# A fused attention and gated-MLP kernel on one core: low parts shared with Pool, turned h from the accumulator, last group on DVE, new tables

## The chip, the cores and the metric

The kernel runs on one core of a Trainium2 chip. The time is that of the device, in microseconds (us), median of several executions. Names of engines: PE is TensorE, ACT ScalarE, DVE VectorE, Pool GpSimd. The mean clock of TensorE, as a share of full speed, is listed for each execution.

## The reference, cut to what matters

```python
def mab(q, kv):                                  # attention of 32 rows over all, or of all over 32
    s = scale * (q @ kv.transpose(0, 2, 1))
    a = np.exp(s - s.max(-1, keepdims=True)); a /= a.sum(-1, keepdims=True) + 1e-09
    return a @ kv
h = mab(I, x)                                    # x: 4 batches of 12416 x 128, I: 32 x 128
x = mab(x, h)
g = x @ w_gate                                   # 128 x 1536
out = x + sigmoid(x @ w_res) * (gelu(g) * (x @ w_val) @ w_out)
```

The kernel never forms the second attention's result ahead of the MLP: with `h` only 32 rows, `h @ w_gate` and `h @ w_val` are made once a batch (`hgv`), and each block of tokens multiplies its 32 weights (`rt`) into them. Batch 0 has nothing to hide behind, so its `h` is made in a prologue, during which no gelu runs.

## The kernel before: the parts that matter here

Each tile of x (1024 tokens) is split into a float16 high part and a float16 low part, is turned on PE, gets its exponentials on ACT, and is accumulated on PE. In the prologue the high parts are cast on DVE or ACT, and all low parts are subtracted on DVE:

```python
def convert_hi(b, k, eng):                       # act: a Copy; else tensor_copy, float32 -> float16
    ...
def convert_lo(b, k, eng):
    po.memset(lo[:, :w, P:P + 1], 1.0)
    eng.tensor_tensor(lo[:, :w, :P], xf, hi, AL.subtract)     # two SBUF inputs
...
for n in range(ntile + 2):
    hi_next(n + 1)                               # ACT for odd tiles below 10, else DVE
    if n < ntile:
        convert_lo(0, tiles[n], ve)
        turn_pe(0, tiles[n])                     # 8 transpositions on PE, copied out by ACT
    if 1 <= n <= ntile: exps("a", 0, ...)        # tile n - 1
    if n >= 2:
        if n == ntile + 1: weight_cast(0, ve); weight_cast(1, ve)
        accumulate(0, ...)                       # tile n - 2; DVE copies the end result to nacc
finish_h(0)      # PE folds nacc; DVE reciprocal and scaling; Pool makes hra of it
turn_h(0)        # PE transposes, DVE copies: ht
for i in range(2, 5): weight_cast(i, po)
exps("b", 0, 0, half, bank_v())
first_layer(0, 0, act)
...
act.activation(gel, parts, AC.Gelu, ...)         # brings the gelu table in (1.28 us on ACT at 35.34)
warm = bank_f()
for i in range(10):
    pe.matmul(warm, wG[:, :P], wG[:, :TOK], start=True, stop=True)
```

The main part is a list of words that say in what order PE, ACT and DVE get their work ("the tables"). A group of 512 tokens ends with `th * ffn + at`, partly on DVE, partly by way of ACT and Pool:

```python
if on_act:
    act.activation(fe, f, AC.Copy, ...)
    po.tensor_tensor(th, th, fe, AL.mult); po.tensor_tensor(at, at, fe, AL.add)
else:
    ve.scalar_tensor_tensor(th, th, 1.0, f, AL.add, AL.mult)
po.tensor_tensor(at, at, th, AL.add)
sy.dma_start(out[...], at)
```

The softmax here doesn't subtract the row's maximum and nothing guards it: scores larger than these inputs give would overflow.

## Time and profile before

| | before |
|---|---|
| median time, range of the first three executions | 776.06 us (775.07 to 777.73) |
| accumulator read by DVE (nacc) | 27.54 us |
| ht begins | 29.40 us |
| first gelu | 37.22 us |
| last product on PE ends | 768.40 us |
| span of the profile | 773.1 us |

The table is read as five points of one road. The stretch to nacc is the first stage, from nacc to the first gelu the second, then come 731.2 us of main part, which is 1164 gelus at 0.63 us each, and a tail of 4.7 us. As a first reading, what delays the first gelu delays everything, because in the main part ACT and DVE are both full (from 200 to 300 us ACT is busy 99.94 of the 100 us, DVE 97.73). The lines for this are in the prediction below.

### The profile page before, as it was taken

To read this page: it belongs to the slowest core of one execution; us is meant where nothing else is said; L and a number is where in the kernel's file an instruction comes from. 1 tells how busy PE (TensorE), PEld (TensorE's weight loads), DVE (VectorE), ACT (ScalarE), POOL (GpSimd) and SP (SyncE) were. 2 spreads that over 40 slices of the span, in tenths; PEclk is the share of its full clock that TensorE was granted. 3 is DMA by queue.
4 is the path that set the end of the run, shared out by engine and by line. 5 is a ranking of instruction groups with operands and counts; after the bars stand their busy time and mean duration, and the time that the engine had idled before them with its cause. 6 is when DMAs were issued, how large, how long until landed. Compare 5 with 4: busy or idle time off the path is not lost.

```text
span 773.1 us, 23909 instructions
## 1 busy us (share of the span) xinstructions
PE 736.8 (95%) x9590; PEld 431.0 (56%) x9590; DVE 742.4 (96%) x737; ACT 754.2 (98%) x1505; POOL 462.5 (60%) x466
## 2 busy tenths in 40 slices
PE   5799999999999999999999999999999999999997
PEld 4555555555655555565655555556565554655554
DVE  7799999989999999999999999998999999999997
ACT  6799999999999999999999999999999999999997
POOL 0238989713598886833377896872267871434155
PEclk9999999999999999999999999999999999999999
DMA  8325596510245675620124485560106341110101
GB/s 339 120 49 122 145 217 162 142 59 29 50 79 117 146 187 149 175 66 30 43 64 99 107 217 144 152 156 29 38 21 129 87 86 43 42 43 29 43 31 58
DMA packets 118449, 78.16 MB, mean 101 GB/s; under 512 B 96672, under 2 KB 99392, under 8 KB 118336
## 3 DMA queue, kind: packets, MB, share of 16 engines
q1 hardware_dynamic: 118336, 76.62, 38.7%
q8 instruction: 75, 1.23, 0.6%
q14 instruction: 38, 0.31, 0.1%
HBM read 27.87 MB, written 25.43 MB: 69 GB/s over the span
## 4 chain that ended last, share of the span: by engine, by line
ACT 43%; PE 39%; issue 11%; DVE 5%; DMA 1%; POOL 1%; SPq 0%; ACTq 0%; POOLq 0%; DVEq 0%
ACT ge L368 29%; PE f L391 18%; PE g L357 10%; PE v L357 6%; ACT th L405 3%; ACT at L410 3%; DVE u L362 3%; PE g L399 3%; ACT e L166 2%; ACT xt L141 1%; ACT fe L419 1%; ACT L166 1%; ACT hi L116 1%; ACT L368 1%; DMA ge<-in_x_dram 1%
## 5 line engine op out<-in xcount | busy, mean ns | idle before, releaser
L362 DVE TENSOR_TENSOR u<-ge,v 128x1024 bf16<-128x1024 f32 x584 | 670.6, 1212 | 10.3 <-PE v L357 2.7
L368 ACT ACTIVATE ge<-g 128x512 f32<-128x512 f32 x1164 | 609.1, 657 | 2.7 <-PE g L357 1.2
L391 PEld LDWEIGHTS <-u 128*128 128x128 bf16 x4656 | 270.1, 98 | 207.8 <-issue 203.4
L391 PE MATMUL f<-wO,u 128*128 128x128 bf16 x4656 | 370.4, 220 | 4.3 <-ACT fe L419 1.1
L357 PE MATMUL g<-rt,hgv 32*128 32x512 f16 x1152 | 335.9, 379 | 9.3 <-ACT ge L368 0.6
L357 PE MATMUL v<-rt,hgv 32*128 32x512 f16 x1152 | 222.9, 385 | 2.5 <-DVE u L362 1.6
L424 POOL TENSOR_TENSOR at<-at,th 128x512 f32<-128x512 f32 (+1 forms) x100 | 124.0, 1240 | 148.2 <-DVE th L423 52.0
L357 PEld LDWEIGHTS <-hgv 32*128 32x128 bf16 x2400 | 73.7, 91 | 87.8 <-issue 24.2
L420 POOL TENSOR_TENSOR th<-th,fe 128x512 f32<-128x512 f32 (+1 forms) x35 | 41.3, 1180 | 94.4 <-ACT fe L419 94.4
L294 POOL TENSOR_TENSOR a<-e,z 128x1024 f16<-128x1024 f32 (+1 forms) x48 | 89.7, 1880 | 12.3 <-DVE z L280 7.8
L124 POOL TENSOR_TENSOR lo<-xf,hi 128x1024 f16<-128x1024 f32 x36 | 76.9, 2136 | 0.2
L399 PE MATMUL g<-hra,rt 128*128 128x128 f16 x768 | 71.3, 219 | 2.5
L405 ACT ACTIVATE th<-g 128x512 f32<-128x512 f32 (+1 forms) x100 | 64.1, 649 | 0.3 <-PE g L399 0.2
L410 ACT ACTIVATE at<-g 128x512 f32<-128x512 f32 (+1 forms) x100 | 64.3, 651 | 0.0
L399 PEld LDWEIGHTS <-rt 128*128 128x128 f16 x768 | 50.7, 97 | 16.1 <-issue 13.1
L118 POOL CAST hi<-xf 128x1024 f16<-128x1024 f32 x36 | 37.3, 1037 | 16.9 <-DMA xf<-in_x_dram 12.5
L423 DVE SCALAR_TENSOR_TENSOR th<-th,f 128x512 f32<-128x512 f32 x65 | 44.4, 683 | 2.5 <-PE g L162 1.8
L421 POOL TENSOR_TENSOR at<-at,fe 128x512 f32<-128x512 f32 (+1 forms) x35 | 41.3, 1179 | 0.0
L162 PEld LDWEIGHTS <-xt 128*128 128x128 f16 x768 | 23.0, 97 | 7.3 <-issue 3.4
L419 ACT ACTIVATE fe<-f 128x512 f32<-128x512 f32 (+1 forms) x35 | 22.1, 631 | 0.9 <-PE f L391 0.9
L273 POOL TENSOR_TENSOR a<-a 128x256 f32<-128x256 f32 (+5 forms) x45 | 18.6, 413 | 3.5
L207 POOL CAST hra<-nacc 64x128 f16<-64x128 f32 x4 | 1.1, 288 | 29.3 <-DVE nacc L200 29.3
(114 smaller groups left out, 280.0 us busy)
## 6 DMA issues: line engine op xcount, KB each, us to landing
out_dram<-at SPq DMA_DIRECT2D x96, 256.0 KB, 2.2
xf<-in_x_dram SPq DMA_DIRECT2D x38, 512.0 KB, 4.5
ge<-in_x_dram SPq DMA_DIRECT2D x10, 512.0 KB, 8.3
rt<-a SPq DMA_TRANSPOSE x48, 3.2
xt<-hi SPq DMA_TRANSPOSE x36, 3.4
ge<-in_moe_w_gate_dram SPq DMA_DIRECT2D x1, 512.0 KB, 8.4
ge<-in_moe_w_val_dram SPq DMA_DIRECT2D x1, 512.0 KB, 8.5
ge<-in_moe_w_out_dram SPq DMA_DIRECT2D x1, 512.0 KB, 4.2
```

The source lines that it names most:

```text
L124: eng.tensor_tensor(lo[:, :w, :P], xf_t.pop((b, k))[:, :w, :], hi_t[b, k][:, :w, :], AL.subtract)
L294: eng.tensor_tensor(a2[:, :n], ev[:, o:o + n, :].unsqueeze(2).to_broadcast([P, n, Q, M]), z[:, o:o + n].unsqueeze(2).unsqueeze(3).to_broad ...
L357: pe.matmul(*t[n], start=True, stop=True)
L362: ve.tensor_tensor(u[:, :n], ge_t.pop(value)[:, :n], v_t.pop(value)[:, :n], AL.mult)
L368: act.activation(ge_t[i][:, h * TOK:h * TOK + n], gb[:, :n], AC.Gelu, bias=0.0, scale=1.0)
L391: pe.matmul(self.ffn[:, k, :], u_t[self.gi, si][:, o:o + P], wO[:, fc, :], start=first, stop=not self.todo, skip_group_check=True)
L399: pe.matmul(bank[:, k * P:(k + 1) * P], rt_t[self.b, self.k][:, self.j0 + k, :], hra_t[self.b][:, s, :], start=True, stop=True)
L405: act.activation(self.th[:, :self.tw], self.mix(0), AC.Tanh, bias=0.0, scale=0.5)
L410: act.activation(self.at[:, :self.tw], self.mix(1), AC.Copy, bias=0.0, scale=1.0)
L420: po.tensor_tensor(th, th, fe, AL.mult)
L423: ve.scalar_tensor_tensor(th, th, 1.0, f, AL.add, AL.mult)
L424: po.tensor_tensor(at, at, th, AL.add)
```

## The change

Its intent was to shorten the prologue by balancing three engines, to shorten the tail, and to anneal the tables once more. The diff, cut (the copy helper of `turn_pe`, the other engine arguments and the 75 rows of tables are left out):

```diff
+    def turned_h(b):
+        hs = bank_g(); na = nacc_t[b]
+        pe.matmul(hs[:, :M], na[:, P:P + 1].to_broadcast([P, P]), strips[:, 0, :], ...)
+        pe.matmul(hs[:, P:2 * P], na[:, :P], strips.rearrange("p q m -> p (q m)"), ...)
+        ve.reciprocal(rz, hs[:, :M])
+        ve.tensor_tensor(ht, hs[:, P:2 * P], rz (broadcast), AL.mult)
...
-            po.tensor_tensor(at, at, th, AL.add)
+            (ve if self.gi == ngrp - 1 else po).tensor_tensor(at, at, th, AL.add)
...
-            convert_hi(0, tiles[n], act if n % 2 and n < 10 else ve)
+            convert_hi(0, tiles[n + 1], ve)
-            convert_lo(0, tiles[n], ve)
+            convert_lo(0, tiles[n], po if w == PRE and n % 2 and n < ntile - 1 else ve)
...
-    finish_h(0)
-    turn_h(0)
+    weight_cast(0, act)
+    weight_cast(1, act)
+    turned_h(0)
     for i in range(2, 5):
         weight_cast(i, po)
-    exps("b", 0, 0, half, bank_v())
-    first_layer(0, 0, act)
+    exps("b", 0, 0, half, bank_g())
+    finish_h(0)
+    first_layer(0, 0)                  # its copy now on DVE
...
-    for i in range(10):
+    for i in range(6):
         pe.matmul(warm, ...)
...
-                lasts.pop(0).end(on_act[lg.gi])
+                lasts.pop(0).end(on_act[lg.gi] and lg.gi < ngrp - 1)
```

Accumulation also runs three tiles behind instead of two.

More of the change, by code (lines that the diff above doesn't have):

```diff
@@ L132, in turn, with turn_pe @@
                                hi_t[b, k][:, :w, :].rearrange("p k c -> p (k c)"))
-    def turn_pe(b, k):
+    def turn_pe(b, k, both=False):
         _, w = blocks_of(k)
@@ L137, in turn_pe @@
         xt_t[b, k] = xt
+        if both:
+            for j0, eng in ((0, act), (w // 2, ve)):
+                tps = bank_g().bitcast(FP16).rearrange("p (k c) -> p k c", c=P)
+                for j in range(j0, j0 + w // 2):
+                    pe.transpose(tps[:, j - j0, :], hi_t[b, k][:, j, :], identF)
+                if eng is act:
+                    act.activation(xt[:, j0:j0 + w // 2, :], tps[:, :w // 2, :], AC.Copy,
+                                   bias=0.0, scale=1.0)
+                else:
+                    eng.tensor_copy(xt[:, j0:j0 + w // 2, :], tps[:, :w // 2, :])
+            return
         tps = bank_g().bitcast(FP16).rearrange("p (k c) -> p k c", c=P)
@@ L210, in finish_h @@
         hgv_t[b] = p_h.tile([P, F], BF16, name="hgv", tag="hgv")
+    def turned_h(b):
+        hs = bank_g()
+        na = nacc_t[b]
+        pe.matmul(hs[:, :M], na[:, P:P + 1].to_broadcast([P, P]), strips[:, 0, :],
+                  start=True, stop=True)
+        pe.matmul(hs[:, P:2 * P], na[:, :P], strips.rearrange("p q m -> p (q m)"),
+                  start=True, stop=True)
+        rz = p_h.tile([P, M], FP32, name="rzt", tag="rzt", bufs=1)
+        ve.reciprocal(rz, hs[:, :M])
+        ht = p_h.tile([P, P], FP16, name="ht", tag="ht")
+        ve.tensor_tensor(ht.rearrange("p (q m) -> p q m", m=M),
+                         hs[:, P:2 * P].rearrange("p (q m) -> p q m", m=M),
+                         rz.unsqueeze(1).to_broadcast([P, Q, M]), AL.mult)
+        ht_t[b] = ht
     def turn_h(b):
@@ L217, in turn_h, with first_layer @@
         ht_t[b] = ht
-    def first_layer(b, c, eng):
+    def first_layer(b, c):
         bank = bank_g()
@@ L222, in first_layer @@
             pe.matmul(bank[r, :], ht_t[b][:, r], w[:, c:c + TOK], start=True, stop=True)
-        if eng is act:
-            act.activation(hgv_t[b][:, c:c + TOK], bank, AC.Copy, bias=0.0, scale=parts)
-        else:
-            ve.tensor_scalar(hgv_t[b][:, c:c + TOK], bank, parts, None, op0=AL.mult)
+        ve.tensor_scalar(hgv_t[b][:, c:c + TOK], bank, parts, None, op0=AL.mult)
     def first_layer_t(b, s):
@@ L248, in spread, with res_layer @@
                                a2[:, :n].rearrange("p c q m -> p (c q m)"))
-    def res_layer(b):
+    def res_layer(b, eng=act):
         bank = bank_g()
@@ L253, in res_layer @@
         hra = hra_t[b]
-        act.activation(hra[:64, 0, :], bank[:64, :P], AC.Copy, bias=0.0, scale=1.0)
+        if eng is act:
+            act.activation(hra[:64, 0, :], bank[:64, :P], AC.Copy, bias=0.0, scale=1.0)
+        else:
+            eng.tensor_copy(hra[:64, 0, :], bank[:64, :P])
         ve.tensor_tensor(hra[M:2 * M, 0, :], bank[M:2 * M, :P], hra[M:2 * M, 0, :], AL.subtract)
@@ L484, in weight_cast @@
         dst, src, w = pieces[i]
-        eng.tensor_copy(dst, staged.pop(i)[:, :w])
+        if eng is act:
+            act.activation(dst, staged.pop(i)[:, :w], AC.Copy, bias=0.0, scale=1.0)
+        else:
+            eng.tensor_copy(dst, staged.pop(i)[:, :w])
     for i in range(len(pieces)):
         weight_in(i)
-    def hi_next(n):
+    convert_hi(0, tiles[0], ve)
+    for n in range(ntile + 3):
+        if n + 1 < ntile:
+            convert_hi(0, tiles[n + 1], ve)
         if n < ntile:
-            convert_hi(0, tiles[n], act if n % 2 and n < 10 else ve)
-    hi_next(0)
-    for n in range(ntile + 2):
-        hi_next(n + 1)
-        if n < ntile:
-            convert_lo(0, tiles[n], ve)
-            turn_pe(0, tiles[n])
+            w = blocks_of(tiles[n])[1]
+            convert_lo(0, tiles[n], po if w == PRE and n % 2 and n < ntile - 1 else ve)
+            turn_pe(0, tiles[n], n == ntile - 1 and w == PRE)
         if 1 <= n <= ntile:
@@ L503 @@
             exps("a", 0, n0, n0 + w, bank_v())
-        if n >= 2:
-            if n == ntile + 1:
-                weight_cast(0, ve)
-                weight_cast(1, ve)
-            n0, w = blocks_of(tiles[n - 2])
-            accumulate(0, n0, n0 + w, n == 2, n == ntile + 1)
-    finish_h(0)
-    turn_h(0)
+        if n >= 3:
+            n0, w = blocks_of(tiles[n - 3])
+            accumulate(0, n0, n0 + w, n == 3, n == ntile + 2)
+    weight_cast(0, act)
+    weight_cast(1, act)
+    turned_h(0)
     for i in range(2, 5):
@@ L514 @@
     half = PRE // 2
-    exps("b", 0, 0, half, bank_v())
-    first_layer(0, 0, act)
+    exps("b", 0, 0, half, bank_g())
+    finish_h(0)
+    hf_t.pop(0)
+    first_layer(0, 0)
     exps("b", 0, half, WIDE, bank_v())
-    later = [(t0, min(t0 + WIDE, nblk)) for t0 in range(WIDE, nblk, WIDE)]
-    exps("b", 0, *later[0], bank_v())
+    exps("b", 0, WIDE, 2 * WIDE, bank_v())
     sums_b(0, 0, half, ve)
@@ L522 @@
     weights_b(0, 0, 0, half, ve, True)
-    for j0, j1 in later[1:]:
-        exps("b", 0, j0, j1, bank_v())
-    first_layer(0, TOK, ve)
-    first_layer(0, 2 * TOK, ve)
-    res_layer(0)
+    first_layer(0, TOK)
+    for j0 in range(2 * WIDE, nblk, WIDE // 2):
+        exps("b", 0, j0, min(j0 + WIDE // 2, nblk), bank_g())
+    first_layer(0, 2 * TOK)
+    res_layer(0, ve)
     sums_b(0, half, WIDE, ve)
@@ L532 @@
         weight_cast(i, po)
+    later = [(t0, min(t0 + WIDE, nblk)) for t0 in range(WIDE, nblk, WIDE)]
     gel = konst.tile([P, 1], FP32, name="gel")
@@ L536 @@
     warm = bank_f()
-    for i in range(10):
+    for i in range(6):
         pe.matmul(warm, wG[:, :P], wG[:, :TOK], start=True, stop=True)
     plan_first = [
-        "GGQGG GVG4 P6 P4 GV R8VG",
-        "G5GQG 7AQ6 RP8A GP6 GQ2 4GQ *",
-        "7P8G Q8 GQ13R P8 4P 5Q",
-        "R7P 8P10 AA6GP 4GQ7 P8 P10",
-        "GGGV 9GQ2G 8RP 1P7 P A8P7G",
-        "Q 13GP 12P Q8GG 7P3 1Q",
-        "R5PA P11 P4 A9V GP5GG 6P",
-        "8P 5A4P QR 10PR 10GP QA14",
-        "P11 QG8 GGV6 GG9RQG 5GQ9 GQ9",
-        "GVG 7GVGR9 GQA9GG Q 5P5G VR10",
-        "P10 P 18EV VEE2Ac cQ5 P *",
-        "10GQ7GG Q7G GV6G Q11AG Q12 P7G",
-        "V G6P4R 7P 6P G6GP Q4R7 *",
-        "P7G Q4A4 V GA9GGV 13PG 7Q",
-        "6GP6 P7 P7G Q8 RR7P A8P",
-        "8GQ 8GQ9A 3P8 R4GQG1 5P6 QG7",
-        "GVG7G Q7A 4P5 R6GP2 GQ7 GQ7GG",
-        "V17EE E15EcP 6cP Q9AR4 P5 GVA7G",
-        "Q6 GGV11 GGcP Q8R P7G P7 *",
-        "QG7 GQ6R 5QG 8hP 4P6A 5GtQ",
-        "QG9l G1QG 6Q G4A7P 6P lGV5RR",
-        "8P 7P7rG V 21EEAV EEEEVE6 9PG17",
-        "GoQ6 QG8 R2GQoG 5VGG 6P5A 6P *",
-        "R8VG G6GVG 12oPG11 oGQ7 GQ5 2P7",
-        "GVG 7A4P5G *",
+        "GGPG P5 P3 GQ8 GGV7GG Q6",
+        "VGR3 2P 7P A7QGG Q8RA 8P",
+        "7P 7P9A P9R GP5 P6 P5G *",
+        "V8 RP11 QG11 2PG 10P7 P10",
+        "R1P8 P8A 4PA5G Q7 Q GQG6GG",
+        "V G5VGG 8P 8GV GR9GGVG QR13A",
+        "GQ5 VGG 8P 9P7G G6Q QA6",
+        "A7GQ 10GQG 9QG7 GG9RVG G5QG9 QG9",
+        "P8 P8 AR9P Q9 GG5Q G7GGV",
+        "6VGG8 GVG3A 10QG GQ3 R10P7 GQ2R",
+        "10P 16EV V E6EcP 6cQ P5G *",
+        "4P 6GVG 6P3A10 2P Q11 R5P",
+        "6P7 P8 AP3 R8PG5G Q7 GQ7G",
+        "VGA9 GQ8 GQ4R 8P PA8 P5",
+        "GGV 8R3P3 Q G7GGV6GG8AG Q6 P3",
+        "6P10 VGG10G Q3A 10GP3G VG9 GQ9",
+        "GQ5R8G Q9 A5RQG 4P8 GQ3E 6EV *",
+        "VE14E ccP7 2VGG4 cGQ5G Q6A6G Q7",
+        "VGG7RhG Q2GG5 tPG10R QG6 Q G7QlA",
+        "6P 7GGV7G GV7G G8RQG 6Q G7GVG",
+        "G6V GG7GQ 7QG 9AR6V GlP A8P7A",
+        "4P 5P 7rQ15 E1EVEE1 EEEQ V18",
+        "P12oA 5P P3R 10RP Q7 GoG7GQ *",
+        "7P A8P7 GQ12 RGQ 11GVG 8GQ8",
+        "GoQ8 P8GGo5G *",
@@ L581 @@
     ]
     plan = [
-        "AP Q7R 5AP8G Q5 1QG5 GQ5R *",
-        "6V GG6P 12GQ G4Q6 P7G P",
-        "6GVG6 P7 RQ5RA 7VGGG5 P7 GQ7G *",
-        "Q8 RQA8 P4 Q9 PA13G VG",
-        "9QG11 GQ2 8A5RP 1P 7GQ7G QA7G *",
-        "Q7 GQ7G VG12 GP12 P 7P7",
-        "GV G7P 8RR7GP VG8G P8 P8A",
-        "1P6 P6 GQ6A 5P P10R 3QG",
-        "9P 9QG10GG 7P P 8RP7 P *",
-        "6QG5 GVG8 AQA14 GQ4 P 6P *",
-        "7PR 7P1 5P 9RP 9GP V12",
-        "P7 A5VGG8G Q7 P6GR 3GV P12GG",
-        "Q6 7GQ8 GQ7 RA8GP 6P8 P9",
@@ L596 @@
-        "GQ7 A6QG8R 4GQ GV5GG 7GQ 7GQ8R",
-        "2P6 P8A 5AP 4GQ 8GQ 8GQ",
-        "R9GQ 19EEEV VE EE6EccQ G9P 7VGG6 *",
-        "A2Q A8P 7QG3 cP6R 2P7 P8",
-        "P8 P7 GQ10AR cP3 P7G Q6",
-        "GG6P 7VGG8G Q11GGc GV2 R3P6Gh GVG2G",
-        "Q10A2 1GQ8G Q8AR 6tP1 GGV 7GVG8A",
-        "1VG R7P7 GGV17E EV VEE1 EE10EP",
-        "Qo30G V G7lGVG VGG6lR 6P7GG V6",
-        "QoG4 3GVG8 AR8GV GPo7GGo5A 6P6 P7",
-        "GQ 8RQ2 GG7rGV G2P11 GQG10 P7",
-        "P8 P5A5 *",
+        "VR P 3AGP 9P A9P 5P *",
@@ new lines @@
+        "7GQ 7P3 R8QR 9Q GGV10A 5P8 *",
+        "QG10 P15 GP5 VG7 GQ7G Q",
+        "4R7QR 6P6 A6V GGQ3 GG7VGG7G Q8AG",
+        "VA 9P 8GG6VGGG 4P 7P 7P6",
+        "P8 P8 RR8P P8 A3P 7P10",
+        "RP8 P6 2GQ 4PG GGVA9G Q8 *",
+        "Q G8GP7G Q 7P G9VG P12",
+        "A4P 3VGG7 P6 1GGV8R R7P Q7A *",
+        "R9P7 P6 QG7 GQ 12P A12QG",
+        "7P 9VG G9P A11RQ GQ7 GG7VGG",
+        "7P7 GVG7G Q7GG6 QGG Q7G GV3",
+        "R8QG 8P7G GV7RA 8PG5G Q9 GQ9",
+        "P8 P9A A8RP 6P 7V GG7GQ7G",
@@ L608 @@
+        "Q7G Q7AR 7GQ Q5GG 8GQ 9P10R",
+        "3QEEE 13V VEEEcE1 cGQ 14P8G Q7 *",
+        "2P 5A8Q G3cV GP6 A5P 8RQR9G *",
+        "Q7 P4A 7P 2cP4 P 6GQ8A",
+        "3P 7GQ2 6P 12GGcGQG hVGG1 P7G",
+        "GV7 R4GVG 7GQ7G Q8 RA7GtGVG VG8",
+        "R4GQ9 GQ8 GQ2 17EEEV VEEE3 3EQ10",
+        "P21o P3A 8PG6 P6 P7 GQ7G",
+        "VG 6A5oP4 R7llGQGoo Q7A4 P5 R6P",
+        "8rGVG 3GQ7AR 8QG Q7G G7GQ7G VG9",
+        "P10 P8GG *",
     ]
     plan_last = [
-        "AP Q5 R7PR2 Q1 A12P 7VGG *",
@@ L611 @@
-        "8P 8GP 10P Q7A6 Q R7P5 *",
-        "P5G 3QG 3GV12 GQG12 P4A VG4",
-        "QR 9P R10GQ A9P GGQ 10QG *",
-        "11GQ8 P7 GQ3R 9Q P13 AP7 *",
-        "P6 2P9 P6 R5P Q13 2P",
-        "9P4 4GVG8R A8P G3P 6P6 A3P1G",
-        "Q6G Q6 P4G Q6GG 7P A1P *",
-        "7P8 P5R 7P 8VGG 12Q P6 *",
-        "R7P7 GGV10 VGGA6 5VG G7P Q13",
-        "GGV8 GVG8A 4GQ 9RQ G6GGQ Q8AR *",
-        "7VGG 11P10 P12 GP V 10AQA8",
-        "QG4 1GP7 Q R8PG 10P P6R",
-        "8P10 P10 P10A 4P P3R 10P",
@@ L624 @@
-        "9P10 QG10 RA6GV GQ7 GG8GVG8G Q6 *",
-        "P6 GQ7 6PG 10QR8 QG7GG V6 *",
-        "QG9 AQ8 P G11P 4P 7P",
-        "7PR 9P A10GQG VG7R 4P3 3QG",
-        "6GQG 6QG4 VGG8 RGQ1A 6P GV7RA *",
-        "8P9 QG10 GQ14 GP 7Q7 P8A4 *",
-        "GQ 8P 14V GP11R GQ5 P6A5 *",
-        "P7 GQ5 1PG 8Q P6 6P4 *",
-        "A7GQ 7RQ2 R7P4 5GQG V13 P7 *",
-        "A6GQ8 GVG6 Q8G GQ15 GQ11G Q10",
-        "GQRA12GG GGGPGG *",
+        "P3 P1 AP Q2 R6GQ G9P *",
+        "7AVG5G Q3R 7P6 P7 R4QG Q13 *",
@@ new lines @@
+        "GQ 9AQR 8P7G GV6 A5QG Q14G",
+        "Q10 P11 GQ3A 10P P7 GG6GQ",
+        "7P6 R3P 6P5R 8AQ P7GG VA7G *",
+        "P7 P 7P7G Q13G P8 VG2 *",
+        "3P 7GVG4R 7P 5P12 PG9 QR *",
+        "8P 7P7 P 6AQ11 RP2 8P *",
+        "7P 3QA 9GQ7 GQ12 P G10VGR",
+        "7QG 7P 7PA 9P8GGG V Q7 *",
+        "RA9GQ 7P 7GVG6 GQ12A P12 P6 *",
+        "RQ7G Q8 P6 R9PG V12 A4QG6",
+        "P7 GQ4R 7PA8 GQ G6P 8GQ *",
+        "8V GG8GV G7GQ11 P A12GQ 7GQ *",
+        "7GQ7 R4QG 11Q GQ11 A3P 6P",
@@ L635 @@
+        "8R2P5 P3 R10AGV G3P6 GP7 GQ6",
+        "P4 2P 7GVG7G GQ 6GV GGQA10R *",
+        "4V GG10GQ 10GQ14A QG12 P7 GQ7 *",
+        "GQ6 1GQ 7R8Q P11G Q7R4 VGG6 *",
+        "QG6R VG4A 6Q 4PG12G Q7 GVG4GG",
+        "V5GG Q5 2GGV7 A6AQ QG7GG 6GQ *",
+        "7P 7P7 P9 R5GP V12 P6 *",
+        "R6P6 P9 AQ9 RP7 Q7 P10A *",
+        "3P8 P 13P 5P 9GQ7 5P11GG",
+        "GGQ RGGAG11GP",
     ]
```

## The prediction

> **What bounds the kernel now.** I read the page's totals first, then the table of windows, then the chain of waits over the first 60 us, then the timeline of the first 48 and last 18 us. The totals say that three engines are nearly full, so the kernel has no single idle resource to fill:
>
> ```profile
> PE 736.8 (95%) x9590; PEld 431.0 (56%) x9590; DVE 742.4 (96%) x737; ACT 754.2 (98%) x1505; POOL 462.5 (60%) x466
> ...
> ACT 43%; PE 39%; issue 11%; DVE 5%; DMA 1%; POOL 1%; SPq 0%; ACTq 0%; POOLq 0%; DVEq 0%
> ```
>
> The reader is to see ACT ahead of DVE by 2% of the span and no DMA in the chain. The windows split the span in three: a prologue up to the first gelu at 37.2 us, a main part to about 768 us, and a tail of 4.6 us in which only Pool and a transfer work:
>
> ```profile
> 200.00:300.00 100.00, 97.47 (x1181) 55.47 (x1177) 97.73 (x94) 99.94 (x205) 82.53 (x80) 1.00 0.56 123
> ...
> 700.00:760.00 60.00, 58.13 (x681) 32.96 (x677) 59.99 (x55) 60.00 (x123) 25.22 (x20) 1.00 0.10 37
> 760.00:768.50 8.50, 7.90 (x117) 5.53 (x116) 7.94 (x8) 7.27 (x17) 4.81 (x4) 1.00 0.18 65
> 768.50:773.10 4.60, 0.00 (x0) 0.00 (x0) 0.00 (x0) 0.21 (x1) 1.56 (x4) 0.78 0.20 73
> ```
>
> Columns are PE, PE load, DVE, ACT, Pool, then clock, DMA share and GB/s. In the main part ACT is idle 2.9 us in all between 37 and 760 us, DVE 15.7 us. The main part is full; what can move lies in the first 37 us, the last 5 us, and in how well the tables pack the middle.
>
> In the prologue the chain is ACT's own queue, one tile after another (start, length):
>
> ```profile
> 16.22 0.94 ACT hi L116
> 17.16 0.91 ACT xt L141
> 18.07 0.28 ACT e L166
> 18.35 0.92 ACT xt L141
> 19.26 0.28 ACT e L166
> 19.54 0.94 ACT hi L116
> ```
>
> Two tiles of x cost ACT 0.94 + 2 x (0.91 + 0.28) = 3.3 us. The last exponential of this stage is at 26.6, the last product into the accumulator at 27.5 (DVE reads it at 27.54), and from there it takes 9.7 us to the first gelu.
>
> [...]DVE's hi casts take 690 ns, its lo subtractions 1221 ns for the same 1024 elements. [...]DVE multiplies two SBUF tensors while Pool casts weights:
>
> ```profile
> 30.88 1.04 POOL L485 CAST wV<-ge 128x1024 bf16<-128x1024 f32 x1
> 30.94 1.52 DVE L294 TENSOR_TENSOR a<-e,z 128x512 f16<-128x512 f32 x1
> 31.86 0.75 POOL L485 CAST wR<-ge 128x128 bf16<-128x128 f32 x1
> ```
>
> DVE's `a` has half the elements of a lo subtraction, so about 0.69 us of its own, yet takes 1.52: it waits some 0.83 us, till Pool's wV is almost done. Pool's wR, 128 elements wide, takes 0.75 where Pool's cast of the same shape takes 0.286 elsewhere: it waits till `a` is almost done. [...]the trace has 1283; both kernels have sixteen loads on ACT, so that term is zero.
>
> **The change part by part.**
>
> *Exponentials only on ACT.* Five hi casts leave ACT (5 x 0.94 = 4.7 us off the chain) and go to DVE (5 x 0.61 = 3.1 us back to back). One transposed tile is shared with DVE. ACT's two tiles would then cost 2 x 1.19 = 2.4 us.
>
> *Low parts shared.* DVE had twelve large lo subtractions; six go to Pool. These are the durations that decide the case:
>
> ```profile
> L124 POOL TENSOR_TENSOR lo<-xf,hi 128x1024 f16<-128x1024 f32 x36 | 76.9, 2136 | 0.2
> ...
> L124 DVE TENSOR_TENSOR lo<-ge,hi 128x1024 f16<-128x1024 f32 x10 | 12.0, 1221 | 0.9 <-ACT hi L116 0.8
> ...
> L118 DVE CAST hi<-ge 128x1024 f16<-128x1024 f32 x6 | 4.1, 690 | 3.2 <-DMA ge<-in_x_dram 3.2
> ```
>
> If Pool worked beside DVE, two tiles would cost DVE 2 x 0.61 + 1.14 = 2.4 us and Pool 2.1: balanced with ACT's 2.4. [...]Then two tiles cost 2.4 + 2.05 = 4.4 us, against 3.3 now. Six pairs make 26.5 us; with 0.7 us in which DVE waits for the second tile's transfer and 0.5 for the small tile, counted from the first cast at 4.8, the last low part comes at about 32.5. Transposing the last tile, its exponentials and the last products add about 2: accumulator complete at about 34.5, 7.0 us later than now. ACT and PE would stand idle in between. The transfers do not decide it: the last x transfer is issued at 10.3 and the longest of them needs 11.5 us, so all x is there by 22.
>
> *h turned from the accumulator.* Now: nacc 27.54, fold on PE, reciprocal, scaling, transposition on PE, copy: ht done at 29.69, 2.15 us. After: copy, two PE products, reciprocal of 32 columns, one multiply: about 0.35 + 0.5 + 0.25 + 0.35 = 1.5. Saves 0.65.
>
> *The rest of the road to the first gelu.* From ht (29.69) to gelu (37.22) are 7.5 us now; ACT is busy 5.8 of them. The hgv copy (0.66) and the hra copy (0.27) leave ACT, four warm-up products (4 x 0.23) leave PE, and exponentials now alternate over the other PSUM buffers. DVE gets the hgv and hra copies. The weight casts on ACT come in while it waits for DVE. [...]I take 0.6 of the 0.9.
>
> *Tail.* Now the small last group goes fe on ACT at 768.43, three Pool steps to 770.18, then the transfer:
>
> ```profile
> 768.43 0.28 ACT L419 ACTIVATE fe<-f 128x128 f32<-128x128 f32 x1 [0.91 <-PE f L391]
> 768.79 0.45 POOL L420 TENSOR_TENSOR th<-th,fe 128x128 f32<-128x128 f32 x1
> 769.20 0.45 POOL L421 TENSOR_TENSOR at<-at,fe 128x128 f32<-128x128 f32 x1
> 769.73 0.45 POOL L424 TENSOR_TENSOR at<-at,th 128x128 f32<-128x128 f32 x1
> ```
>
> After, DVE does two steps of about 0.28 each. 1.75 us becomes 0.65: saves 1.1.
>
> *Tables.* The instruction counts of the main part do not change (1164 gelus, 584 `u`, 35 groups closed on ACT in both), so only packing can gain. 2.9 us of visible ACT gaps and 15.7 of DVE's are the room; the tables were annealed before. I take 2.0, the least supported term.
>
> Sum: +7.0 - 0.65 - 0.6 - 1.1 - 2.0 = +2.7, so 778.7 us.
>
> **The rivals.**
>
> *Rival A, Pool works beside DVE.* For it: the change was evidently laid out on this assumption (2.4 on ACT, 2.4 on DVE, 2.1 on Pool, the accumulation put back one tile for Pool's latency), and main-part Pool times are steady beside a busy DVE. Against it: DVE's main operation `u` reads one operand from PSUM, so that steadiness proves nothing for two SBUF inputs, and the one place with two of them shows the wait. Under A the accumulator is complete at about 24.8 (2.7 earlier than now), limited by ACT and the transfers: 776.1 - 2.7 - 0.65 - 0.6 - 1.1 - 2.0 = 769.0.
>
> *Rival B, a partial lock.* [...]only some of the 12 us of Pool work is added. With half of it, two tiles cost 3.4, as now: accumulator at about 28, total about 772.
>
> *Rival C, the tables matter more than the prologue.* ACT's gelus take 523 ns each of busy time where undisturbed runs of nine take about 490; thus some 30 us of short waits hide inside busy time. A good annealing could find 5 of them, a table fitted to a start that the chip does not deliver could lose 3. That moves any of the above by -3 to +5.
>
> **Range and chances.** I give the full lock about 65%, A 20%, B 15%; C spreads each by about 3 us. Most of the mass is between 776 and 782, a lesser part at 768 to 773. My time is 778.5 us, range 768.0 to 783.0. Two per cent is 15.5 us, more than any of these sums reach: faster 0.02, same 0.96, slower 0.02.
>
> **What would show it.** In the profile after: DVE hi or lo in the prologue taking 2 us or more instead of 0.69 and 1.22, and Pool's lo well over 2.14, with the last accumulation at 33 to 35 us: the lock. Unchanged durations and an accumulation before 26: A. The gap from nacc to ht near 1.5 and from ht to first gelu near 6.9 test the two road terms; fewer than 4 us from last PE product to the end tests the tail; the length from first gelu to the last product, 731 us now, tests the tables. I am wrong if the lock is not there, or if the main part shortens by more than 5 us.

No term of the sum is among them: it still comes to +7.0 - 0.65 - 0.6 - 1.1 - 2.0 = +2.7, so 778.7 us. That DVE's casts and subtractions and Pool's subtractions take turns, so that Pool's 2.05 us add to DVE's 2.4, was the estimate. In the trace of before DVE's `a` took 1.52 us beside Pool's casts (the same instruction takes 0.69 in the changed kernel at 40.43 us, while Pool is idle). "Lock" stands for this, here and below: instructions of DVE and Pool take as long as if they had taken turns. Taking 0.6 of the 0.9 us on the way to the first gelu was an estimate, too. The 1283 is ns of one table load on ACT (`ACT_TABLE_LOAD`, 16 in the traces of both kernels).

## The result, and the profile after

The changed kernel took 784.26 us (783.84 to 786.85, four executions) beside 775.91 us of the kernel before. The ratio is 1.0111 (95% interval 1.0083 to 1.0140). Ratios are the mean time of one kernel's fast runs over that of the other's of the same rounds, so not quite the ratio of the medians. It is slower by about 8.4 us, in the direction that was expected and beyond the range; this is clear of the noise. The profiled execution is the slowest of the four.

| | before | after | difference |
|---|---|---|---|
| nacc | 27.54 | 35.35 | +7.8 |
| ht begins | 29.40 | 37.35 | |
| first gelu | 37.22 | 46.10 | +8.9 |
| last product on PE ends | 768.40 | 781.47 | +13.1 |
| span | 773.1 | 785.0 | +11.9 |

Four things are to be seen. **First, DVE and Pool lengthen each other's instructions.** The timeline of the changed kernel in the prologue (start, length, engine, line, operation; an idle time before it in brackets):

```profile
8.18 2.15 DVE L118 CAST his<-ge 128x128 f16<-128x128 f32 x1
...
14.33 1.21 DVE L124 TENSOR_TENSOR lo<-ge,hi 128x1024 f16<-128x1024 f32 x1
14.49 3.04 POOL L124 TENSOR_TENSOR lo<-ge,hi 128x1024 f16<-128x1024 f32 x1 [1.22 <-DVE hi L118]
15.47 3.26 DVE L118 CAST hi<-ge 128x1024 f16<-128x1024 f32 x2
...
18.65 1.21 DVE L124 TENSOR_TENSOR lo<-ge,hi 128x1024 f16<-128x1024 f32 x1
...
30.58 1.52 POOL L516 CAST wG<-ge 128x1024 bf16<-128x1024 f32 x1
...
31.24 1.93 DVE L124 TENSOR_TENSOR lo<-ge,hi 128x1024 f16<-128x1024 f32 x1
32.05 2.03 POOL L516 CAST wV<-ge 128x1024 bf16<-128x1024 f32 x1
```

Pool's low part is issued while DVE is in its own; it takes 3.04 us instead of 2.14. DVE's next two casts then take 3.26 us instead of 1.30. The lengths fit turns: from the end of DVE's low part (15.54) to the end of Pool's (17.53) are 1.99 us, and from there to the end of DVE's two casts (18.73) 1.20. A cast of an eighth of the size takes 2.15 us instead of 0.22; it ends at 10.33, and the low part of Pool beside it (7.22, 3.03 us long) at 10.25. The cycle of two tiles is 18.65 - 14.33 = 4.32 us. None of the added time is listed as idle: it stands inside the busy time (DVE counts as busy for 10.00 of the 10 us from 20 to 30). (The 1.22 in brackets is Pool waiting for the high part to be cast.) The last three lines are a second case of the same thing, which the prediction did not see: Pool's weight casts now begin when the last low part is due.

**Second, TensorE's clock.** The table of windows of the changed kernel (PE, PE load, DVE, ACT, Pool, granted clock, DMA share, GB/s):

```profile
20.00:30.00 10.00, 6.76 (x160) 5.33 (x159) 10.00 (x7) 6.71 (x12) 7.55 (x7) 0.94 0.33 111
30.00:40.00 10.00, 7.27 (x133) 5.67 (x134) 5.69 (x10) 2.76 (x7) 5.37 (x9) 0.50 0.27 80
40.00:45.00 5.00, 4.41 (x80) 2.84 (x77) 3.17 (x7) 3.96 (x6) 0.05 (x1) 0.75 0.01 3
...
50.00:57.00 7.00, 7.00 (x57) 3.55 (x53) 5.75 (x5) 5.65 (x11) 1.39 (x1) 0.50 0.20 39
```

PE was idle a third of the time from 20 to 30 us, and its clock was granted at half from 28.9 to 42.5 and from 49.3 to 59.6. Before, the half clocks on record in the first 60 us were 3.4 us at 30.4 and 3.4 at 40.6. Idle time alone does not tell the two apart: before, PE was idle for 2.9 of the same 10 us, against 3.2 here, and kept its clock; the section on why the prediction was wrong comes back to this. The column also hides a part. The trace has no record of the clock ahead of 22.0 us here and of 13.3 us before, and the column then says 1.00 (as the mean clocks of the executions count it), but eight transpositions took 1.03 us up to there and 0.62 afterwards, in both kernels, so PE was slow from the start:

```profile
19.88 1.03 PE L152 MATMUL g<-identF,hi 128*128 128x128 f16 x8
...
22.56 0.62 PE L152 MATMUL g<-identF,hi 128*128 128x128 f16 x8 [0.87 <-DVE hi L118]
```

In the traces all half clocks ahead of the very end last 3.4, 6.8, 10.2 or 13.7 us, and the executions of one kernel differ (mean clock 0.975 to 0.987 in the four of the changed kernel). What the clock goes with is taken up below.

**Third, the second stage** did not get shorter:

```profile
35.35 0.29 DVE L199 COPY nacc<-f 128x129 f32<-128x129 f32 x1 [1.84 <-PE f L194]
...
36.95 0.36 DVE L233 RECIPROCAL rzt<-g 128x32 f32<-128x32 f32 x1 [1.31 <-PE g L230]
37.35 0.29 DVE L235 TENSOR_TENSOR ht<-g,rzt 128x128 f16<-128x128 f32 x1
...
40.07 1.94 ACT L178 ACTIVATE e<-v 128x896 f32<-128x896 f32 x2 [1.70 <-PE v L174]
```

DVE waits 1.31 us for the two float32 products, and ACT 1.70 us for exponents (from 39.10) that stand in PE's queue behind the postponed fold (37.82) and the first layer (38.53), all at half clock.

**Fourth, the tail** is shorter, as planned; two steps of DVE stand where ACT and three steps of Pool stood:

```profile
781.58 0.29 DVE L451 SCALAR_TENSOR_TENSOR th<-th,f 128x128 f32<-128x128 f32 x1 [0.56 <-PE f L419]
782.07 0.29 DVE L452 TENSOR_TENSOR at<-at,th 128x128 f32<-128x128 f32 x1 [0.21 <-DVE th L451]
```

From the last product to the end: 3.5 us instead of 4.7.

### The profile page after: what moved, and what is told of

Same layout as the page of the kernel before. It is cut to its first block, busy times and chain, and to the rows that moved or that the text cites. A ratio compares the mean times of both kernels' runs of the same rounds, so it can differ in the third digit from the quotient of the medians.

```text
span 785.0 us, 23909 instructions
## 1 busy us (share of the span) xinstructions
PE 747.4 (95%) x9589; PEld 439.1 (56%) x9589; DVE 753.5 (96%) x739; ACT 750.6 (96%) x1501; POOL 483.2 (62%) x471
## 5 line engine op out<-in xcount | busy, mean ns | idle before, releaser
L390 DVE TENSOR_TENSOR u<-ge,v 128x1024 bf16<-128x1024 f32 x584 | 672.6, 1212 | 11.9 <-PE g L385 3.4
L419 PEld LDWEIGHTS <-u 128*128 128x128 bf16 x4656 | 274.3, 99 | 208.7 <-issue 204.1
L419 PE MATMUL f<-wO,u 128*128 128x128 bf16 x4656 | 375.8, 222 | 4.3 <-DVE th L451 0.5
L124 POOL TENSOR_TENSOR lo<-xf,hi 128x1024 f16<-128x1024 f32 x37 | 79.9, 2159 | 1.5 <-DVE hi L118 1.2
L451 DVE SCALAR_TENSOR_TENSOR th<-th,f 128x512 f32<-128x512 f32 (+1 forms) x65 | 44.1, 678 | 4.2 <-PE f L419 2.8
L153 ACT ACTIVATE xt<-g 128x1024 f16<-128x1024 f16 x11 | 11.3, 1025 | 12.7 <-PE g L152 11.9
L178 ACT ACTIVATE e<-g 128x512 f32<-128x512 f32 (+2 forms) x39 | 19.7, 603 | 3.8 <-PE g L174 3.7
```

The source lines that it names most:

```text
L124: eng.tensor_tensor(lo[:, :w, :P], xf_t.pop((b, k))[:, :w, :], hi_t[b, k][:, :w, :], AL.subtract)
L390: ve.tensor_tensor(u[:, :n], ge_t.pop(value)[:, :n], v_t.pop(value)[:, :n], AL.mult)
L419: pe.matmul(self.ffn[:, k, :], u_t[self.gi, si][:, o:o + P], wO[:, fc, :], start=first, stop=not self.todo, skip_group_check=True)
```

## The experiments

All outputs are right.

### Low parts back on DVE: a_lo_dve

```diff
-            convert_lo(0, tiles[n], po if w == PRE and n % 2 and n < ntile - 1 else ve)
+            convert_lo(0, tiles[n], ve)
```

> The changed kernel with all low parts on DVE. [...]Pool reads nothing in the prologue until the weight casts, so no wait is left; two tiles cost DVE 2 x 0.61 + 2 x 1.14 = 3.5 us instead of 4.4, the accumulator is complete (DVE's nacc copy) at 28 to 29 us instead of 35.35, DVE's small his cast takes 0.2 us instead of 2.15, and the time falls by 6 to 8 us to about 777. Rival (there is no lock worth mentioning; the prologue is slow because DVE took over the hi casts): with more work on DVE it gets slower still, by about 6 x 1.1 us, to about 791.

Measured: 779.6 us (778.0 to 782.1), ratio to before 1.0058. nacc came at 28.88. The timeline of its prologue has the durations back:

```profile
8.03 0.22 DVE L118 CAST his<-ge 128x128 f16<-128x128 f32 x1
8.16 1.22 DVE L124 TENSOR_TENSOR lo<-ge,hi 128x1024 f16<-128x1024 f32 x1
9.30 0.69 DVE L118 CAST hi<-ge 128x1024 f16<-128x1024 f32 x1
```

Though DVE has more work, the accumulator is complete 6.5 us earlier. That decides between lock and no lock: the rival's 791 is out by far. But the time fell by 4.7 us only, and 1.0058 was left to explain.

### One part alone on the kernel before: b_lo_pool

```diff
-            convert_lo(0, tiles[n], ve)
+            convert_lo(0, tiles[n], po if blocks_of(tiles[n])[1] == PRE and n % 2 and n < ntile - 1 else ve)
```

> The kernel before with one part of the change: the six large low parts of odd tiles on Pool. [...]two tiles cost DVE and Pool together 0.61 + 1.14 + 2.05 = 3.8 us where ACT needs 3.3, and the last two pairs, whose hi casts are all on DVE, 4.4: accumulator complete 3 to 4 us later than 27.5, at 30.5 to 31.5, and 778 to 779 in all. Without a lock DVE has half a low part less per tile and ACT stays the bound: accumulator at 27.5 or sooner, time 775 or less.

Measured: 780.3 us, ratio 1.0056 (1.0041 to 1.0071); nacc at 32.13, 4.6 us later than before. The lock shows from the other side as well: DVE's high parts beside Pool took 2.61 to 2.68 us instead of 0.69, one low part 3.03 instead of 1.22. Of the 4.6 us, 3.7 had been lost when the last low part ended (30.06 instead of 26.34), which is the 3 to 4 expected; the other 0.9 comes after it, while PE's clock fell to half at 31.3. Whether that is the cause was not tested.

### The tables alone: a_old_tables and b_new_tables

The edit exchanges the three tables, nothing else.

> The changed kernel with the tables of the kernel before. First gelu to last product of PE was 731.2 us before and 735.4 in the changed kernel's slowest, profiled run. If the new tables are the cause of that: 731 to 732 us here and a time of 781 to 782. If a late start and a throttled PE cause it, or chance: 784 plus or minus 1. If the new tables are better, as the prediction had it: 786.

> The kernel before with the new tables, all else as before. Tables worse in themselves: 777 to 779. Tables better by the 2 us of the prediction: 774. Tables fit only the prologue that they were made for: slower than before, while the run with the old tables in the changed kernel is not faster than the changed kernel.

Measured: the changed kernel with the old tables 783.7 us, ratio 1.0112, against 1.0111 with the new. Its profile has a main part of 731.9 us instead of 735.4, as expected if the tables lose it, but the median did not follow: the changed kernel's profile is of its slowest execution. The kernel before with the new tables 775.4 us, ratio 1.0003 (0.9979 to 1.0026). The tables are worth nothing on the average. But the executions of b_new_tables are spread as those of before are not, and follow the clock: 772.7 us at a mean clock of 0.993, 773.3 at 0.990, 774.7 at 0.989, 776.2 at 0.987, 776.4 at 0.984, 779.3 at 0.979. So the new order is shorter by some 2 us where the clock holds, and the clock holds less often. Of all profiles, each of the six with new tables has half clocks in the middle of the main part (after at 285, 469 and 609 us, b_new_tables at 458 and 598), and none of the twelve with old tables has one there.

### Filler products to hold the clock: a_pe_warm, a_pe_warm2

```diff
         bank = bank_g()
+        for _ in range(3):                       # ahead of each tile's transpositions
+            pe.matmul(bank, identF, hi_of_tile_0, start=True, stop=True)
...                                              # 2 ahead of the fold, 3 ahead of the exponentials "b";
+                                                # a_pe_warm2: 10 more in the waits for the last tile
```

The fillers' results are overwritten. Theory 2 puts the part of the loss that the lock leaves down to TensorE's clock. That the clock fell because PE was idle was the estimate.

> The changed kernel with filler products on PE (three of 128x512 before the transpositions of each tile from the fourth on, two ahead of the fold, three ahead of the second exponentials), whose results are overwritten. Theory 2: [...]TensorE's clock, which was granted at half from 29 to 43 us and from 49 to 60[...]. Then with the fillers the clock stays whole, nacc to ht falls from 2.3 to about 1.5 us, ht to first gelu from 8.5 to 7 to 7.5, and the time by 2 to 3 us, to 781 to 782; the accumulator is complete as late as before the fillers, 35 us. Rival (these stretches are long because of DVE's and PE's queues): no change, 784.

> As the first filler run, with ten more filler products in the two waits for the last tile, after which the clock had still fallen (33.6 to 37.0 us). One execution of the first filler run had a mean clock of 0.997 and took 778.4 us, the five others 0.984 to 0.992 and 781 to 785. If the clock is what separates them, the fillers now hold it over the first 50 us more often and the median falls to 779 to 781, with 778 to 779 wherever the mean clock is 0.995 or more[...]. If that one execution was chance: 783 as before, whatever the clock.

Measured: a_pe_warm 782.8 us, ratio 1.0092, with one execution of 778.4 at a clock of 0.997 and five of 781.3 to 784.8 at 0.984 to 0.992. a_pe_warm2 784.0 us, ratio 1.0118, none above 0.987: a miss. Its profile shows why it does not answer the question that it was made for. The clock was whole to 42.2 us, and nacc to the end of ht then took 1.78 us; but the clock fell right there, on the six warm-up products (2.68 us, 0.42 each), the first gelu waited 1.87 us for them, and 10.2 us at half followed from 49.0. The clock can be held for a stretch; more fillers did not make the kernel faster. In the profile of a_pe_warm the clock was at half from 33.5 to 37.0: nacc to the end of ht took 2.48 us, a miss, and from there to the first gelu, all at whole clock, 7.53 us, as in the kernel before.

### The tail alone: b_tail

```diff
+            (ve if self.gi == ngrp - 1 else po).tensor_tensor(at, at, th, AL.add)
+                lasts.pop(0).end(on_act[lg.gi] and lg.gi < ngrp - 1)
```

> The kernel before with only the last small group ended on DVE. From the traces: last product on PE to the end of the span was 4.73 us before and 3.52 in the changed kernel, so 1.2 us less, 773.8 to 774.2 beside 775.0. If the end is set by an earlier, larger store still on its way, nothing: 775.

Measured: 776.2 us beside 775.6, ratio 0.9998 (0.9981 to 1.0015). Two groups again: 774.15 and 774.19 at a clock of 0.995 and 0.994, the others 776.2 to 777.2 at 0.989 to 0.991; before at 0.994 had 774.6 to 775.1. At equal clock the gain is about 0.7 us. The profile fell on the longest execution (777.2 us) and shows how the clock costs time here (the ten warm-up products, then the first gelu):

```profile
35.29 3.75 PE L538 MATMUL f<-wG 128*128 128x512 bf16 x10
39.40 2.06 ACT L368 ACTIVATE ge<-g 128x512 f32<-128x512 f32 x4 [2.21 <-PE v L357]
```

ACT had its gelu table at 37.18 and stood waiting 2.21 us, because the gates stand in PE's queue behind warm-up products that ran at half clock, 0.42 us each.

### The second stage alone: b_road

First stage and tables of before, all else of the change.

> The first stage of the kernel before (hi casts split with ACT, all low parts on DVE) and its tables, but everything else of the change: turned h from the accumulator, hgv copies on DVE, weight casts on ACT, the new order of exponentials, six warm-up products, the last group on DVE. As the prediction had it, the road from accumulator to first gelu saves 1.25 us and the tail 1.1: 772.7. As the run with low parts on DVE suggests (accumulator to first gelu 10.8 us there against 9.7 before), the road costs 1.1 more and the tail gives 1.2 back: 775, with accumulator to first gelu 10.5 to 11.

Measured: 776.0 us, ratio 0.9996 (0.9980 to 1.0011); nacc to first gelu 10.9 us in the profile. At clocks of 0.995 and 0.997 it took 774.5 and 774.1. Second stage and tail together are worth nothing in the median: the stage costs what the tail gives.

### Turned h alone: b_turned_h, and with two repairs: b_warm4, b_th2

> The kernel before with only h turned straight from the accumulator. The prediction: 0.65 us less from nacc to ht (2.15 to 1.5). The traces since: nacc to ht was 2.29 in the changed kernel and 2.3 with the fillers, because the two float32 products on PE take longer than the fold and the transposition did. Then no gain: nacc to ht 2.0 to 2.3 and a time of 775 plus or minus 0.5; if the prediction's size holds at a whole clock, 774.4 or less.

Measured: 776.35 us, ratio 1.0010 (0.9994 to 1.0026), and nacc already late, at 28.77. The cause is in its timeline:

```profile
22.93 1.46 POOL L501 CAST wG<-ge 128x1024 bf16<-128x1024 f32 x1 [21.12 <-DMA ge<-in_moe_w_gate_dram]
23.42 1.53 DVE L118 CAST hi<-ge 128x1024 f16<-128x1024 f32 x1
```

In the kernel before, Pool's weight casts stood in Pool's queue behind the hra copies and so began at 29.9. The edit put them ahead of these copies; they began as soon as the weights had landed, beside DVE's last casts and low parts. The two repairs: four warm-up products instead of ten (with the tail), and then turned h with the casts behind the copies again.

```diff
-    for i in range(10):
+    for i in range(4):                           # b_warm4 and b_th2
...
+    turned_h(0); exps("b", 0, 0, half, bank_v()); finish_h(0); hf_t.pop(0)
+    for i in range(2, 5): weight_cast(i, po)     # b_th2
```

> The kernel before with the tail on DVE and four warm-up products instead of ten. With the tail alone it took 774.2 where ten warm-up products ran at a whole clock and 776.3 in the executions where they ran at half (0.42 instead of 0.23 us each), and then the first gelu waited for them until 39.4. If the queue of warm-up products is the wait: first gelu 36.9 to 37.3 in every execution, median 774.0 to 774.5 and little spread. If they are needed to raise the clock: the early main part runs at half clock and it takes 776 or more.

> As the last, with h turned from the accumulator, and Pool's three weight casts kept behind the hra copies. With turned h alone those casts began at 22.9 us, beside DVE's last hi and low parts, a hi cast took 1.53 us, and the accumulator was complete at 28.77 instead of 27.54. [...]with the casts out of the way it is complete at 27.5 to 27.8 again, and the time is that of the run with four warm-up products or up to 0.4 us less. If something else in that edit made it late: 28.7 again.

Measured: b_warm4 774.6 us, ratio 0.9989 (0.9973 to 1.0004). The first gelu came at 37.58 though the clock was at half from 31.5 to 45.1; where the clock was at 0.995, 773.9 to 774.2 us. b_th2 774.8 us, ratio 0.9996 (0.9979 to 1.0012): nacc at 27.47, so it was the casts; nacc to the end of ht 1.78 us instead of 2.15; first gelu at 36.39, 0.8 us sooner than before. The time shows little of that 0.8: the main part of this profile is 1.2 us longer than before (732.4 instead of 731.2), so an earlier first gelu does not shorten the whole by as much.

### Fillers on the kernel before, and what was left of the change: b_fill, best_old, best_new

> The kernel before with fillers alone: a few ahead of the fold, the transposition of h, the second exponentials and the first turned weights, two ahead of each early gate while the first ffn bank is free, and seven warm-up products instead of ten. Before had half a clock from 30.4 to 33.8 and from 40.6 to 44.0 us. If that costs it time: first gelu 0.4 to 0.8 us sooner, no half clock after 40 us, 774.0 to 774.6 beside 775.3, and fewer slow executions of 776 to 778. If those stretches are bound by DVE and ACT anyway: 775.3.

> What is left of the change that pays, without shared low parts: the kernel before with turned h, the last group on DVE, fillers, old tables. Tail -0.7 at equal clock, turned h -0.36 at a whole clock, fillers -0.5 to -1: 773.3 to 774. If the gains are only those of single traces: 775 to 776.

> The same with the new tables. In the kernel before these took 772.7 at a mean clock of 0.993 and up to 779.3 at 0.979, 775.4 in the median. If the clock lost at the start pulls the later losses after it: 771 to 772. If the new tables lose the clock by themselves in the middle (half clock near 285, 460 and 600 us in three runs so far): median 774, with a spread of several us that follows the clock.

Measured: b_fill 776.8 us (776.6 to 777.0), ratio 1.0015; best_old 778.6, ratio 1.0037; best_new 777.75 (774.9 to 780.5), ratio 1.0024. All missed. From its first clock record at 14.8 us on, b_fill has no half clock before the very end, and a spread of 0.4 us, so fillers do hold the clock; but my own fillers cost more than that was worth. Two of them ahead of each early gate made the gates come at 0.86 us instead of 0.50 (timeline of b_fill, fillers at L366, gates at L370):

```profile
36.64 0.61 PE L366 MATMUL f<-wG 128*128 128x512 bf16 x2
36.75 0.60 ACT L381 ACTIVATE ge<-g 128x512 f32<-128x512 f32 x1 [0.16 <-PE g L370]
37.18 0.38 PE L370 MATMUL g<-rt,hgv 32*128 32x512 f16 x1
37.50 0.60 PE L366 MATMUL f<-wG 128*128 128x512 bf16 x2
37.60 0.60 ACT L381 ACTIVATE ge<-g 128x512 f32<-128x512 f32 x1 [0.26 <-PE g L370]
```

best_old and best_new had, besides, Pool's casts too early. No version beat the kernel before beyond doubt; b_warm4 comes nearest.

### Where the other half went: a_lo_dve_old, twice

The changed kernel, low parts on DVE, old tables; the second time one look only.

> The changed kernel with all low parts on DVE and the tables of before. With the new tables it was 0.58% slower than before, though its first gelu came only 2.4 us later and its tail was 1.2 shorter, with half clocks at 278, 418 and 603 us and a main part of 735 us. If the new tables lose the rest by losing the clock: main part 731 to 732 here, 776 to 777 in all. If not, 779.6 again.

> The same kernel again (changed kernel, low parts on DVE, old tables), for a profile of its usual state: of seven executions one took 774.3 us at a mean clock of 0.997, six 778.1 to 779.8 at 0.985 to 0.989; the profile fell on the one. If TensorE's clock is the other half of the loss, this profile has a clock of 0.985 to 0.99, half clock in more windows within the first 60 us than the single one of 3.4 us at 29.9 in the fast one, and its 4 to 5 us lie in those windows, with the main part after 60 us as long as in the fast profile. If the time is lost elsewhere, the stretch before 60 us is equal in both.

Measured: 774.3 us in one execution at a clock of 0.997, 778.1 to 779.8 in six at 0.985 to 0.989; ratio of all 1.0043. The expected 776 to 777 was missed by the median, 779.0, though the main part of the profile is 730.1 us. The second look gave 775.2 us at 0.995, a fast one again, so no profile of the usual state of this very kernel exists. The two looks still are one program at two clocks: at half for 3.4 us in the first 60 us of the first (from 30.2), for 6.8 us in the second (from 28.0). The second is 1.0 us longer, all of it ahead of the first gelu: nacc at 29.20 instead of 28.70, nacc to the end of ht 2.30 us instead of 1.78, and from there 8.05 us in both, with 3.1 and 3.4 us of it at half clock. The main parts are equal (730.05 and 730.08). For the larger loss, what can be set side by side is the second look and the profile of a_lo_dve, whose first gelus come within 0.12 us of each other (39.55 and 39.67). The windows of the gelus alone, a_lo_dve first (busy us, count, clock):

```profile
0.00:60.00 60.00, 16.14 (x31) 0.86 0.46 163
```

```profile
0.00:60.00 60.00, 18.21 (x36) 0.94 0.47 164
```

At 60 us the kernel whose clock was at half from 42.8 to 53.0 had made 31 gelus, the other 36. Five gelus at 0.63 are 3 us. ACT's timeline of a_lo_dve shows that it waits for gates on PE in that stretch:

```profile
46.47 1.09 ACT L396 ACTIVATE ge<-g 128x512 f32<-128x512 f32 x2 [0.70 <-PE v L385]
47.87 1.58 ACT L396 ACTIVATE ge<-g 128x512 f32<-128x512 f32 x3 [0.32 <-PE v L385]
```

These two kernels differ in their tables too, so the 3 us are not the clock's beyond all doubt; the same program at two clocks (774.3 against 778.1 and more) says that the clock goes with a loss of that size.

## Why the prediction was wrong

**The step that decided the sign was right.** The estimate that Pool's work adds to DVE's, "Then two tiles cost 2.4 + 2.05 = 4.4 us": measured 4.32. Accumulator 7.0 us later: measured 7.8. The 0.8 is mostly Pool's cast of wG, which made DVE's last low part take 1.93 us instead of 1.22; no term had it. Rival A was refuted by b_lo_pool and a_lo_dve, rival B by the same 4.32, where it had 3.4. None of the signs that the prediction named for being wrong came: the lock is there (casts and low parts of 2.15, 3.04 and 3.26 us), and the main part did not shorten.

**The step that failed is the deduction of 3.25 us** for turned h (0.65), the rest of the road (0.6) and the tables (2.0). Measured in the profiles:

| term | predicted | measured (786.9 us, the slowest) | in a_old_tables (783.3 us) | note |
|---|---|---|---|---|
| accumulator complete | +7.0 | +7.8 | +7.5 | |
| nacc to end of ht | -0.65 | +0.14 | +0.14 | 2.29 us at half clock; 1.78 at whole clock in b_th2, a gain of 0.37 |
| ht to first gelu | -0.6 | +0.93 | +0.93 | 8.46 instead of 7.53 |
| main part | -2.0 | +4.2 | +0.7 | tables change nothing in the medians |
| tail | -1.1 | -1.2 | -0.9 | |
| sum | +2.7 | +11.9 | +8.4 | +8.4 in the medians of the changed kernel |

The last column of figures has the old tables, so it has no gain of tables to find; its sum is that of a usual execution.

The three deductions were priced as if PE's clock stayed as it was in the kernel before: whole from nacc to ht, and at half for 3.4 us on the way to the first gelu. The prediction even says that "ACT and PE would stand idle in between" and stops there. PE lost its clock, from 28.9 us through more than half of the second stage and again for 10 us of the main part's start. Counted in gelus: at 60 us the changed kernel had 21, before 38; 17 at 0.63 are 10.7 us, of which 8.9 are the later first gelu and 1.8 came after it. Between 100 and 700 us it lost four more gelus, 2.5 us, with half clocks at 285, 469 and 609; the tail gave 1.2 back.

The test that the prediction set for itself, ht to first gelu "near 6.9", failed with 8.46. Part of that is order, not clock: the fold and the first layer now stand ahead of the exponentials in PE's queue. The two looks at a_lo_dve_old give the share: with 3.1 and 3.4 us of that stretch at half clock, as in the kernel before (3.4), the changed order took 8.05 us and the old one 7.53, so about 0.5 of the 0.93 goes with the order; the other 0.4 comes where 4.9 us are at half clock. b_road, with a first stage as quick as before, gained nothing from nacc to gelu either. Rival C named the tables, -3 to +5, but not the mechanism by which they could lose. Two slips in the working change nothing: ACT was busy 5.65 of the 7.53 us, not 5.8, and 1164 gelus at 33 ns are 38 us, not 30.

**What the clock goes with** can be read from the 18 kept traces; no run was made to test it. Count each product on PE as its columns, times its share of the largest form in the traces, `128*128`: a gate (`32*128 32x512`) counts 512 / 4 = 128, a product with wO (`128*128 128x128`) counts 128 as well. The weight is the author's reckoning. In the trace of the kernel before four gates start within 0.010 us, from 36.795, and the next at 37.021, while the warm-up products of 512 columns on `128*128` start 0.216 us apart. Cut each trace, up to 768 us, into stretches of 3.41 us as its clock records begin and end. Of the stretches at whole clock, 44 were followed by half clock, and these hold 1510 to 3118 such columns; 3842 were followed by whole clock, and only 7 of these hold 3118 or fewer (a usual stretch of the main part has about 4900). Here float32 products count like the others; counted four times, the bound is 3697 and the exceptions are 123, so the margin depends on it. (In the kernel before, two float32 records of 129 columns start 0.214 us apart, at 27.89, and float16 transpositions of 128 columns 0.056 us apart, at 20.6.) PE's busy share tells less: ahead of the half clocks of the main part it was 0.75 to 0.95, because a gate keeps PE busy as long as a warm-up product (both 0.38 us in the kernel before) and counts a quarter of it. This separates the tables. From 100 to 760 us the emptiest 3.41 us hold 2072 to 2074 columns in all six profiles with the new tables, near 600 us, where all six lost the clock; in the twelve with the old tables they hold 3034 to 3162, and none lost it. By this reading the new order bunches gates without their share of wO products, and pays in clock what it wins in packing.

**What stays open.** That the clock is the main part of the loss that the lock leaves is supported by executions of one program (a_pe_warm, a_lo_dve_old, b_new_tables) and by places in the traces where ACT waits for PE at half clock. It was not shown by giving the clock back: fillers held it in b_fill and lost more elsewhere, and in a_pe_warm2 it fell later. Nor was a table annealed that keeps this count up, which would test it. Nor is it known which engine goes first where DVE and Pool meet. In a_lo_dve Pool's cast of wG began at 24.38 us, beside a cast of DVE, and took 3.79 us instead of 1.04, while two more low parts of DVE (24.91 to 27.27) took 2.36, no longer than undisturbed; in the changed kernel Pool's low part (14.49 to 17.53) ended 1.20 us ahead of DVE's casts (15.47 to 18.73). What decides this was not tested.

## What to carry to other kernels

Before sharing work between DVE and Pool, look in a trace at the instructions that will run beside each other. Here DVE's casts of float32 to float16 (3.26 us for two instead of 1.30) and its subtractions (1.93 instead of 1.22) were lengthened beside Pool's subtractions and weight casts, Pool's subtractions were as well (3.04 instead of 2.14), and the sum of both engines counted (4.32 us for two tiles), not the longer one (2.4 as the prediction estimates it). The same came from casts that slid forward in Pool's queue (b_turned_h: 1.53 us for a cast instead of 0.69). Wherever a change will thin out PE's products, price what follows at half of PE's clock as well as at the whole: here the half clock followed on stretches of at most 3118 columns in 3.41 us, by the count above. And compare executions by their clock, not only by their median: a gain of 2 us can hide behind a clock that changes by one per cent (b_new_tables: 772.7 us at 0.993, 776.4 at 0.984).
